# A rebuilt attention pipeline in front of a soft mixture of experts: head pairs, token-major output, wide loads, weights behind attention

## The chip, the cores and the metric

One core of one Trainium2 chip. The metric is the device time of one execution in microseconds (us), of which medians are quoted. For one core a run counts as slow when it is more than 1.5% above the fastest of the same kernel.

## The reference, cut to what matters

Attention over 8 batches and 8 heads, 576 tokens of 64 elements, with 16 extra "beacon" keys that every token sees. Its result is laid out as 4,608 tokens of 512 and goes through a soft mixture of experts: every token is dispatched to 32 slots (8 experts of 4 slots), and each token's output is a mix of all 32 slots.

```python
k_all = np.concatenate([beacon_k, k], axis=2)          # 16 + 576 keys
scores = (1 / np.sqrt(D)) * np.matmul(q, k_all.transpose(0, 1, 3, 2))
scores = np.where(causal, -1e9, scores)                # beacons are never masked
a = softmax(scores)
x = np.matmul(a, v_all).transpose(0, 2, 1, 3).reshape(B * S, H * D)   # 4608 x 512

logits = x @ phi                                       # 4608 x 32
slot_input = softmax(logits, axis=0).T @ x             # 32 x 512
for e in range(8):                                     # 4 slots per expert
    h = np.maximum(slot_input[e] @ w1[e], 0.0)         # 512 x 1024
    slot_out[e] = h @ w2[e]                            # 1024 x 512
out = softmax(logits, axis=1) @ slot_out               # 4608 x 512
```

q, k and v are drawn with a scale of 0.1, so the scores are near zero and the softmax is nearly uniform.

## The kernel before: the parts that the argument touches

All matmuls of attention work on q and k with the head's 64 elements on the partitions, so q and k, which are loaded with tokens on the partitions, are transposed by TensorE. The transposes land in PSUM, and VectorE copies them to SBUF. Two heads (a pair) share one such tile, one on partitions 0 to 63 and one on 64 to 127.

```python
# loads: tokens on partitions, one row of 64 floats (256 B) per token and head
nc.sync.dma_start(out=qs[s][0:rows, i, :, :],
                  in_=q[b, :, i * P:i * P + rows, :].rearrange("h p d -> p h d"))
# ... (k, v and the beacons alike)

for (st, dstT, nch) in ((qs[sb], qTp, NQC), (ks[sb], kTp, NCH)):
    tp = ps_tr.tile([P, nch * P], BF, name="trps", tag="trps")
    for c in range(nch):                       # five transposes of 128 x 128
        hi = st[:, c, hA:hB + 1, :].bitcast(BF).rearrange("p a b -> p (a b)")[:, 1::2]
        nc.tensor.transpose(tp[:, c * P:(c + 1) * P], hi, idb[:, :])
    nc.vector.tensor_copy(out=dstT[:, 0:nch * P], in_=tp[:, :])     # L196: flat on both sides

# ... scores, exp (ScalarE), causal mask (GpSimd) ...

avps = ps_av.tile([P, 1024], FP, name="av", tag="av")
# ... output of attention, transposed: 65 partitions (64 elements and the sum), tokens along columns
nc.tensor.matmul(avps[0:DD, ocol:ocol + w], vsh[sb][:, c, hh, :], expT[:, o:o + w],
                 start=(jj == 0), stop=(jj == len(grp) - 1))                      # L236
# ... copied to SBUF, transposed back by TensorE, divided by the sum

# ... the experts: all weights are loaded after attention
```

The parameters are F = 1,024 for the experts; `BF` is bf16, `F16` fp16 and `FP` fp32.

The softmax here doesn't subtract the row's maximum and nothing guards it: scores larger than these inputs give would overflow.

Of the kernel before, what the change touches and what calls it, by code (L numbers as in the profile page):

```python
# [8 lines left out]
DBG = {}  # L10


def _dbg(nc, name, ap):
    if DBG.get("on"):
        t = nc.dram_tensor(f"dbg_{name}", ap.shape, ap.dtype, kind="ExternalOutput")
        nc.sync.dma_start(out=t.ap(), in_=ap)
        DBG[f"dbg_{name}"] = True


FP = mybir.dt.float32  # L20
F16 = mybir.dt.float16
AL = mybir.AluOpType
AF = mybir.ActivationFunctionType


@with_exitstack
def kernel(
# [12 lines left out]
    nc = tc.nc  # L40
    P = 128

    B, H, S, D = q.shape
    Nb = beacon_k.shape[2]
    SK = S + Nb
    NCH = (SK + P - 1) // P
    SKPAD = NCH * P
    NQC = (S + P - 1) // P
    SQPAD = NQC * P
    Sl = S - (NQC - 1) * P  # L50
    DD = D + 1
    XDD = DD + (DD % 2)
    XT0, XT1 = 704, 1472
    scale = 1.0 / (D ** 0.5)

# [3 lines left out]
    N = out.shape[0]  # L59
    NDC = Dm // P  # L60
    NFC = F // P
    assert Dm == H * D and N == B * S

    SQS = [0, 288, 432, 512, S]
    rects = []
    halves = []
    off = 0
    for hhi in range(len(SQS) - 1):
        a, bnd = SQS[hhi], SQS[hhi + 1]
        ecb = off  # L70
        poff = 0
        idxs = []
        for c in range(NCH):
            sq0 = max(a, max(0, P * c - Nb))
            if sq0 >= bnd:
                continue
            w = bnd - sq0
            idxs.append(len(rects))
            rects.append((c, sq0, w, off, hhi, poff))
            off += w  # L80
            poff += w
        halves.append((idxs, poff, ecb))
        assert poff <= 512
    EXPW = off
    qk_pieces = [(c, hhi, po_, po_ + w, sq0)
                 for (c, sq0, w, o, hhi, po_) in rects]
    half_exp_regions = [[(0, pw, ecb)] for (_i, pw, ecb) in halves]

    mask_regs = []
    for (c, sq0, w, o, hhi, po_) in rects:  # L90
        C = sq0 + Nb - P * c
        if C < 128:
            mw = min(w, 128 - C)
            if mw > 0:
                mask_regs.append((o, mw, C, hhi))

    AVS = 288
    av_spans = [(0, 0, AVS), (512, AVS, S)]

    nchunks = []  # L100
    for b in range(B):
        for i in range(NQC):
            cnt = P if i < NQC - 1 else Sl
            nchunks.append((b, i, b * S + i * P, cnt))

    const = ctx.enter_context(tc.tile_pool(name="const", bufs=1))
    xpool = ctx.enter_context(tc.tile_pool(name="xpool", bufs=1))

    idf = const.tile([P, P], FP, name="idf")
    make_identity(nc, idf)  # L110
    idh = const.tile([P, P], F16, name="idh")
    make_identity(nc, idh)
    idb = const.tile([P, P], mybir.dt.bfloat16, name="idb")
    make_identity(nc, idb)
    ones32 = const.tile([P, 1], FP, name="ones32")
    nc.vector.memset(ones32[:, :], 1.0)
    ones32h = const.tile([P, 1], F16, name="ones32h")
    nc.vector.memset(ones32h[:, :], 1.0)
    phif = const.tile([P, NDC, NSL], FP, name="phif")
    nc.sync.dma_start(out=phif[:, :, :],  # L120
                      in_=moe_phi.rearrange("(c p) e -> p c e", p=P))
    phih = const.tile([P, NDC, NSL], F16, name="phih")
    nc.vector.tensor_copy(out=phih[:, :, :], in_=phif[:, :, :])

    xb = [xpool.tile([P, NQC, H, D], F16, name=f"x_{b}") for b in range(B)]
    eLh = xpool.tile([P, N], F16, name="eLh")
    dsum9 = xpool.tile([P, N // 512], FP, name="dsum9")
    xTes = ExitStack()
    xtp = xTes.enter_context(tc.tile_pool(name="xtp", bufs=1, side="right"))
    xT = [xtp.tile([P, N], F16, name=f"xT_{t}") for t in range(NDC)]  # L130

    with tc.tile_pool(name="stag", bufs=1) as stag, \
         tc.tile_pool(name="pairp", bufs=3) as pairp, \
         tc.tile_pool(name="headp", bufs=3) as headp, \
         tc.tile_pool(name="ps_sc", bufs=4, space=bass.MemoryType.PSUM) as ps_sc, \
         tc.tile_pool(name="ps_av", bufs=1, space=bass.MemoryType.PSUM) as ps_av, \
         tc.tile_pool(name="ps_tr", bufs=2, space=bass.MemoryType.PSUM) as ps_tr:

        qs = [stag.tile([P, NQC, H, D], FP, name=f"qstag{i}") for i in range(2)]
        ks = [stag.tile([P, NCH, H, D], FP, name=f"kstag{i}") for i in range(2)]  # L140
        vs = [stag.tile([P, NCH, H, DD], FP, name="vstag", tag="vstag") for i in range(2)]
        vsh = [stag.tile([P, NCH, H, DD], F16, name=f"vstagh{i}") for i in range(2)]
        oTs = [stag.tile([P, SQPAD], F16, name=f"oT{i}") for i in range(2)]
        vs = [vs[0], vs[0]]
        for i in range(2):
            nc.vector.memset(oTs[i][:, S:SQPAD], 0.0)
            nc.vector.memset(qs[i][64:P, NQC - 1, :, :], 0.0)
            nc.vector.memset(ks[i][64:P, NCH - 1, :, :], 0.0)
            nc.vector.memset(vs[i][:, :, :, D], 1.0)
            nc.vector.memset(vs[i][64:P, NCH - 1, :, :], 0.0)  # L150
            nc.vector.memset(vs[i][64:P - (SKPAD - SK), NCH - 1, :, D], 1.0)

        def stage_batch(b):
            s = b % 2
            for i in range(NQC):
                rows = P if i < NQC - 1 else Sl
                nc.sync.dma_start(
                    out=qs[s][0:rows, i, :, :],
                    in_=q[b, :, i * P:i * P + rows, :].rearrange("h p d -> p h d"))
            nc.sync.dma_start(out=ks[s][0:Nb, 0, :, :],  # L160
                              in_=beacon_k[b].rearrange("h n d -> n h d"))
            nc.sync.dma_start(out=vs[s][0:Nb, 0, :, 0:D],
                              in_=beacon_v[b].rearrange("h n d -> n h d"))
            for c in range(NCH):
                lo = max(0, c * P - Nb)
                hi = min(S, (c + 1) * P - Nb)
                if lo >= hi:
                    continue
                p0 = lo + Nb - c * P
                nc.sync.dma_start(  # L170
                    out=ks[s][p0:p0 + hi - lo, c, :, :],
                    in_=k[b, :, lo:hi, :].rearrange("h p d -> p h d"))
                nc.sync.dma_start(
                    out=vs[s][p0:p0 + hi - lo, c, :, 0:D],
                    in_=v[b, :, lo:hi, :].rearrange("h p d -> p h d"))
            nc.vector.tensor_scalar(out=vsh[s][:, :, :, :], in0=vs[s][:, :, :, :],
                                    scalar1=1.0, scalar2=None, op0=AL.mult)

        stage_batch(0)
        lg_done = [0]  # L180
        for b in range(B):
            if b + 1 < B:
                stage_batch(b + 1)
            sb = b % 2
            for g in range(H // 2):
                hA, hB = 2 * g, 2 * g + 1
                qTp = pairp.tile([P, SQPAD], mybir.dt.bfloat16, name=f"qT_{b}_{g}", tag="qT")
                kTp = pairp.tile([P, SKPAD], mybir.dt.bfloat16, name=f"kT_{b}_{g}", tag="kT")
                BF = mybir.dt.bfloat16
                for (st, dstT, nch) in ((qs[sb], qTp, NQC), (ks[sb], kTp, NCH)):  # L190
                    tp = ps_tr.tile([P, nch * P], BF, name="trps", tag="trps")
                    for c in range(nch):
                        hi = st[:, c, hA:hB + 1, :].bitcast(BF).rearrange(
                            "p a b -> p (a b)")[:, 1::2]
                        nc.tensor.transpose(tp[:, c * P:(c + 1) * P], hi, idb[:, :])  # L195
                    nc.vector.tensor_copy(out=dstT[:, 0:nch * P], in_=tp[:, :])  # L196
                expTs = {}
                for (hh, po) in ((hA, 0), (hB, 64)):
                    expTs[hh] = headp.tile([P, EXPW], F16, name="expT", tag="expT")
                for hhi, (idxs_, pw, ecb) in enumerate(halves):  # L200
                    sct = {}
                    for (hh, po) in ((hA, 0), (hB, 64)):
                        scps = ps_sc.tile([P, 512], FP, name="sc", tag="sc")
                        sct[hh] = scps
                        for (c, hx, plo, phi_, sqlo) in qk_pieces:
                            if hx != hhi:
                                continue
# [91 lines left out]
    with tc.tile_pool(name="moe", bufs=1) as moe, \  # L299
# [20 lines left out]
        for _e in range(3):  # L320
            fetch_expert(_e)
# [133 lines left out]
```

## Time and profile before

| what | before |
|---|---|
| median of 3 runs | 468.28 us (466.35 to 468.69) |
| attention, 32 head pairs | 19 to 340 us of a span of 464.3 |
| experts, with the load of all weights | 340 to 424 us |
| output | 424 to 464 us |
| DMA packets under 512 B | 115,744 of 132,682 |

The page's first part gives each engine's busy time, its share of the span and its instructions. PE is TensorE, PEld its weight loads, DVE is VectorE, ACT is ScalarE and POOL is GpSimd. For the kernel before:

```profile
PE 353.5 (76%) x3360; PEld 234.2 (50%) x3360; DVE 235.1 (51%) x849; ACT 156.2 (34%) x319; POOL 115.2 (25%) x522
```

The chain of waits, followed back from the last instruction, by engine and then by line, of the kernel before:

```profile
PE 65%; ACT 12%; DVE 10%; issue 6%; SPq 3%; POOL 1%; DMA 1%; DVEq 0%; ACTq 0%; POOLq 0%
PE av L236 19%; PE sc L208 17%; ACT expT L216 8%; PE sop L391 5%; PE trps L195 4%; PE av L250 4%; PE hps L371 4%; PE lgps L290 3%; PE fps L411 3%; PE xttr L281 3%; ACT osb L419 3%; ACT hsb L380 2%; POOL expT L222 1%; DVE w1h_5512 L313 1%; DVE w1h_5510 L313 1%
```

The table of stages gives the busy time of each engine in a stretch of time, the granted TensorE clock (1.00 is full speed), the busy share of the DMA engines and what they moved. The stretches are attention, the start of the weight loads, the rest of the experts, and the output; the kernel before:

```profile
core 0: us, PE busy (x) PEld busy (x) DVE busy (x) ACT busy (x) POOL busy (x), PEclk, DMA share, GB/s
20.00:340.00 320.00, 271.63 (x2996) 203.37 (x2995) 172.73 (x686) 122.37 (x272) 113.67 (x512) 0.63 0.39 89
340.00:358.00 18.00, 15.42 (x78) 5.97 (x78) 12.62 (x44) 1.69 (x4) 0.00 (x0) 1.00 1.03 411
358.00:424.00 66.00, 41.56 (x184) 14.19 (x185) 32.07 (x28) 7.09 (x7) 0.00 (x0) 0.77 0.87 347
424.00:464.00 40.00, 19.82 (x72) 8.20 (x71) 11.48 (x72) 23.38 (x36) 0.00 (x0) 0.55 0.63 236
```

In attention TensorE is busy 85% of the time (271.6 of 320 us), at a mean clock of 0.63, and no other engine reaches 55%. TensorE bounds this stage. DMA is idle for more than half of it, and the weights come only after it, at 411 GB/s with the DMA full.

VectorE's copies of the transposed q and k, two of them in the view of one line (columns: duration in ns as minimum/median/maximum, the first and last start in us, the shape):

```profile
L196 DVE COPY qT_0_177<-trps x1: 492/492/492, 9.1 to 9.1; 128x640 bf16<-128x640 bf16 x1
L196 DVE COPY kT_1_324<-trps x1: 480/480/480, 18.8 to 18.8; 128x640 bf16<-128x640 bf16 x1
```

A flat copy of 640 two-byte elements per partition from PSUM to SBUF takes 0.48 us. There are two per pair.

### The profile page before, as it was taken

How to read it: one execution, taken by the hardware profiler on the slowest of the kernel's cores; microseconds unless marked ns; L12 is line 12 of the kernel's file. 1: busy time of each engine (PE TensorE's matmuls, PEld its weight loads, DVE VectorE, ACT ScalarE, POOL GpSimd, SP SyncE). 2: the span in 40 equal slices, each digit the busy share in tenths (PEclk: the TensorE clock that was granted, in tenths of full speed). 3: DMA queues.
4: the chain of work that ended last, by engine and by line, in shares of the span. 5: the costliest groups of instructions: out<-in, count | busy, mean ns of one | idle time of the engine just before them, and what ended most of it. 6: DMA issues, size and time to landing. Idle time of an engine off the chain costs nothing.

```text
span 464.3 us, 8865 instructions
## 1 busy us (share of the span) xinstructions
PE 353.5 (76%) x3360; PEld 234.2 (50%) x3360; DVE 235.1 (51%) x849; ACT 156.2 (34%) x319; POOL 115.2 (25%) x522
## 2 busy tenths in 40 slices
PE   2597699988988888897897898895798566665563
PEld 1376576666666666666676666664333212222221
DVE  3244544465464465566665546445456644472331
ACT  1254233334343343435434334441010011003663
POOL 1253242224243243344434424331000000000000
PEclk9995555566665585579576567557589966769555
DMA  8993093077067086077260000000499999960776
GB/s 191 234 235 76 6 230 81 0 156 159 1 145 168 1 189 124 2 158 157 56 154 1 3 1 1 1 1 0 183 388 414 413 416 416 416 250 18 266 275 256
DMA packets 132682, 72.46 MB, mean 156 GB/s; under 512 B 115744, under 2 KB 115744, under 8 KB 132640
## 3 DMA queue, kind: packets, MB, share of 16 engines
q1 hardware_dynamic: 132640, 71.90, 52.1%
q8 instruction: 26, 0.43, 0.4%
q14 instruction: 16, 0.13, 0.1%
HBM read 62.46 MB, written 9.44 MB: 155 GB/s over the span
## 4 chain that ended last, share of the span: by engine, by line
PE 65%; ACT 12%; DVE 10%; issue 6%; SPq 3%; POOL 1%; DMA 1%; DVEq 0%; ACTq 0%; POOLq 0%
PE av L236 19%; PE sc L208 17%; ACT expT L216 8%; PE sop L391 5%; PE trps L195 4%; PE av L250 4%; PE hps L371 4%; PE lgps L290 3%; PE fps L411 3%; PE xttr L281 3%; ACT osb L419 3%; ACT hsb L380 2%; POOL expT L222 1%; DVE w1h_5512 L313 1%; DVE w1h_5510 L313 1%
## 5 line engine op out<-in xcount | busy, mean ns | idle before, releaser
L216 ACT ACTIVATE expT<-sc 128x496 f16<-128x496 f32 (+3 forms) x256 | 117.9, 519 | 187.2 <-PE av L236 129.0
L222 POOL TENSOR_SCALAR_AFFINE_SELECT expT<-expT 128x64 f16<-128x64 f16 (+5 forms) x512 | 113.7, 261 | 201.6 <-ACT expT L216 201.5
L236 PE MATMUL av<-expT,vstagh_125 128*65 128x64 f16 (+6 forms) x544 | 47.6, 259 | 3.7 <-DVE x_84 L269 2.5
L236 PE MATMUL av<-expT,vstagh_126 128*65 128x64 f16 (+6 forms) x544 | 47.2, 261 | 3.4 <-DVE xT_99 L283 1.4
L236 PEld LDWEIGHTS <-vstagh_125 128*65 128x65 f16 x544 | 42.3, 153 | 9.7 <-issue 4.8
L236 PEld LDWEIGHTS <-vstagh_126 128*65 128x65 f16 x544 | 42.8, 155 | 8.4 <-PE xttr L281 2.8
L243 DVE CAST oT_128<-av 65x288 f16<-65x288 f32 x32 | 14.5, 454 | 47.2 <-PE av L236 47.0
L380 ACT ACTIVATE hsb<-hps 4x1024 f16<-4x1024 f32 x8 | 8.1, 1013 | 71.7 <-PE hps L371 55.7
L243 DVE CAST oT_127<-av 65x288 f16<-65x288 f32 x32 | 14.5, 454 | 34.5 <-PE av L236 34.5
L411 PE MATMUL fps<-soh,eLh 32*128 32x512 f16 x36 | 19.7, 551 | 14.6 <-ACT osb L419 13.7
L419 ACT ACTIVATE osb<-fps,rc 128x512 f32<-128x512 f32 x36 | 23.4, 686 | 14.9 <-PE fps L413 6.8
L371 PEld LDWEIGHTS <-siT 128*4 128x4 f16 x64 | 5.5, 95 | 24.9 <-DVE w1h_5510 L313 6.8
L195 PE MATMUL trps<-idb,qstag_119 128*128 128x128 bf16 x80 | 10.6, 268 | 8.0 <-DMA qstag_119<-in_q_dram 7.6
L416 DVE TENSOR_SCALAR rc<-fps 128x1 f32<-128x1 f32 x36 | 5.7, 157 | 21.5 <-PE fps L413 20.7
L195 PE MATMUL trps<-idb,kstag_121 128*128 128x128 bf16 x80 | 10.9, 262 | 7.0 <-DMA kstag_121<-in_k_dram 6.2
L250 PE MATMUL av<-idh,oT_127 65*128 65x65 f16 x160 | 13.5, 230 | 3.1 <-DVE oT_127 L245 3.0
L250 PE MATMUL av<-idh,oT_128 65*128 65x65 f16 x160 | 12.8, 223 | 2.8 <-DVE oT_128 L245 2.8
L293 ACT ACTIVATE eLh<-lgps 32x512 f16<-32x512 f32 x9 | 5.3, 584 | 28.1 <-PE lgps L290 28.1
L245 DVE CAST oT_127<-av 65x288 f16<-65x288 f32 x32 | 14.2, 444 | 0.0
L245 DVE CAST oT_128<-av 65x288 f16<-65x288 f32 x32 | 14.2, 444 | 0.0
L250 PEld LDWEIGHTS <-oT_127 65*128 65x128 f16 x160 | 9.4, 118 | 7.3 <-DVE oT_127 L243 2.3
L283 DVE COPY xT_100<-xttr 128x128 f16<-128x128 f16 (+1 forms) x40 | 8.4, 211 | 8.4 <-PE xttr L281 8.1
(559 smaller groups left out, 592.8 us busy)
## 6 DMA issues: line engine op xcount, KB each, us to landing
out_dram<-osb SPq DMA_DIRECT2D x9, 1024.0 KB, 4.3
w1s_5506<-in_moe_w_dram SPq DMA_DIRECT2D x4, 2048.0 KB, 9.9
w2s_5508<-in_moe_w_dram SPq DMA_DIRECT2D x4, 2048.0 KB, 12.8
w1s_5507<-in_moe_w_dram SPq DMA_DIRECT2D x4, 2048.0 KB, 10.8
w2s_5509<-in_moe_w_dram SPq DMA_DIRECT2D x4, 2048.0 KB, 13.0
vstag<-in_v_dram SPq DMA_DIRECT2D x24, 256.0 KB, 4.5
qstag_119<-in_q_dram SPq DMA_DIRECT2D x16, 256.0 KB, 4.6
qstag_120<-in_q_dram SPq DMA_DIRECT2D x16, 256.0 KB, 4.3
```

What stands on the lines that cost most here:

```text
L195: nc.tensor.transpose(tp[:, c * P:(c + 1) * P], hi, idb[:, :])
L208: nc.tensor.matmul(scps[:, plo:phi_], kTp[po:po + D, c * P:(c + 1) * P], qTp[po:po + D, sqlo:sqlo + (phi_ - plo)], start=True, stop=True)
L216: nc.scalar.activation(expT[:, elo:elo + (bhi - blo)], sct[hh][:, blo:bhi], AF.Exp, scale=scale)
L222: nc.gpsimd.affine_select(out=expT[:, mlo:mlo + mw], in_=expT[:, mlo:mlo + mw], compare_op=AL.is_ge, fill=0.0, base=C, pattern=[[1, mw]], ...
L236: nc.tensor.matmul(avps[0:DD, ocol:ocol + w], vsh[sb][:, c, hh, :], expT[:, o:o + w], start=(jj == 0), stop=(jj == len(grp) - 1))
L243: nc.vector.tensor_copy(out=oT[0:DD, sa0:sb0], in_=avps[0:DD, ob0:ob0 + (sb0 - sa0)])
L245: nc.vector.tensor_copy(out=oT[0:DD, sa1:sb1], in_=avps[0:DD, ob1:ob1 + (sb1 - sa1)])
L250: nc.tensor.transpose(xth[:, base:base + DD], oT[0:DD, i * P:(i + 1) * P], idh[0:DD, 0:DD])
L371: nc.tensor.matmul(hp[0:SPE, fh * 512:(fh + 1) * 512], siT[:, t, e * SPE:(e + 1) * SPE], w1h[se][:, t, fh * 512:(fh + 1) * 512], start=(t ...
L391: nc.tensor.matmul(sop[0:NSL, :], hTz[e % 2][:, t, :], w2h[se][:, t, :], start=(e == 0 and t == 0), stop=(e == E - 1 and t == NFC - 1))
L411: nc.tensor.matmul(fp_[:, 0:Dm], eLh[0:NSL, nbase:nbase + P], soh[0:NSL, :], start=True, stop=True)
L419: nc.scalar.activation(osb[:, j, :], fp_[:, 0:Dm], AF.Copy, scale=rc[:, 0:1])
```

## The change

The intent is to take work from TensorE, to use the idle DMA during attention, and to issue fewer and larger instructions.

- q and k of a head pair are loaded as one block. Partition p gets nine consecutive tokens, 2,304 B in one row, instead of nine rows of 256 B.
- Nine pairs of 64x64 transposes replace five of 128x128 for each of q and k. Since a partition holds consecutive tokens, transpose j yields the tokens j, j+9, j+18 and so on; the copy to SBUF puts them back in order.
- Scores and exponentials work on two PSUM banks (both heads) at once: four exponentials per pair.
- The attention output is computed with tokens on the partitions, so it needs no transposes back. Both heads accumulate in one tile.
- The routing (logits, dispatch) is cut into pieces and run between the pairs. Of the 32 weight pieces, 14 are loaded and 13 cast to fp16 during attention.
- The output is taken out of PSUM by ScalarE and VectorE together.

The diff, cut to its core (cuts marked with `...`):

```diff
-                nc.sync.dma_start(
-                    out=qs[s][0:rows, i, :, :],
-                    in_=q[b, :, i * P:i * P + rows, :].rearrange("h p d -> p h d"))
+            nc.sync.dma_start(
+                out=t[:, :, :],
+                in_=src[b, 2 * g:2 * g + 2].rearrange("h s d -> (h s) d").rearrange(
+                    "(p j) d -> p j d", j=J))                                  # J = 9
...
-                    for c in range(nch):
-                        ...
-                        nc.tensor.transpose(tp[:, c * P:(c + 1) * P], hi, idb[:, :])
-                    nc.vector.tensor_copy(out=dstT[:, 0:nch * P], in_=tp[:, :])
+            for j in range(J):
+                for po in (0, 64):
+                    hi = t[po:po + 64, j, :].bitcast(BF)[:, 1::2]
+                    nc.tensor.transpose(tp[po:po + 64, j, :], hi,              # L203
+                                        idb[po:po + 64, po:po + 64])
+            nc.vector.tensor_copy(                                             # L205
+                out=dst[:, Nb:Nb + S].rearrange("p (s j) -> p j s", j=J), in_=tp[:, :, :])
...
+    av = ps_av.tile([P, 2, 512], FP, name="av")                # one tile, both heads, made once
...
-                                nc.tensor.matmul(
-                                    avps[0:DD, ocol:ocol + w],
-                                    vsh[sb][:, c, hh, :],
-                                    expT[:, o:o + w], ...)
-                    ... copy, transpose back, divide ...
+                nc.tensor.matmul(                                              # L244
+                    av[0:m, a, i * DD:(i + 1) * DD],
+                    ex[n][0:kn, a, o:o + m],
+                    vh[b % 2][0:kn, c, h, :],
+                    start=(c == 0), stop=(c == i))
+        nc.vector.reciprocal(out=r5[:, :], in_=avv[:, :, D])                   # L251
+        nc.vector.tensor_tensor(out=xb[b % 2][:, :, h, :], ...)                # L252
...
+        if n + 1 < NP:
+            transp(n + 1)          # the copies of the next pair are issued ...
+        if n >= 1:
+            attend(n - 1, 0)       # ... ahead of the division of this one, on VectorE
...
+            if n % 2 == 1 and n >= 5 and wl < 16 + 3:
+                load_w(wl)         # one weight piece of 1 MB every second pair
```

## The prediction

> **What bounds the kernel now.** The page and the table of stages split the 464 us span: first score matmul at 19.0 us, attention to 340, experts to 424, output to 464.
> - Attention, 321 us for 32 head pairs, about 10 us each, is bound by TensorE: busy 86%, while DVE has 55%, ACT 38%, POOL 36%, DMA 0 to 57%. The granted clock there is 0.57 to 0.63. Successive matmuls start 240 ns apart for 288 columns, 1.2 columns/ns. Per pair, with routing, about 7 us of streaming at half clock; the rest waits: ACT's exps wait for the output matmuls (129 us in the waits).
> - Experts: DMA busy 0.87 to 1.03 at 411 GB/s; 33.6 MB of weights come only now.
> - Output: 36 ACTIVATEs of 0.69 us, about 1.1 us apart, 236 GB/s.
>
> **What the change does.**
> 1. Attention output token-major: 30 matmuls of 65 columns per pair instead of 3,328 + 650 columns, no copy of the transposed output. At half clock 54 ns each: 1.6 us against 3.3.
> 2. q/k transposes: 36 of 64x64. Couples lie on disjoint quarters of the array; estimate 75 ns (55 to 110) per couple: 1.35 us against 1.07.
> 3. Scores still about 1,680 columns per couple: 1.4 us.
> 4. Routing 5.4 us per batch: 1.35 us per pair.
> 5. ACT: four two-bank exps, estimated from 0.597 us per 512 and 0.579 per 496 as 0.83 ns/column + 0.17: 3.5 us per pair against 4.15. DVE about 3.7 us, POOL about 2.5 us.
> So TensorE needs 6.2 to 7.2 us per pair at half clock, 4.5 at full clock (then DVE and the exp chain limit). Output matmuls fill 128 columns instead of 65 and idle time shrinks, so I expect more full clock: mean 0.65 to 0.7. TensorE: Matmul & The Clock Gate (Trainium skill), Part 1, gives two states set by activity; the trace agrees (only 0.5 and 1.0, in multiples of 3.4 us), but not which work raises it. Estimate 5.5 us per pair, attention about 178 us against 321.
> 6. Loads: q/k rows become 2,304 B. DMA: Bandwidth & Descriptors, Specifications, asks for 512 B at line rate; the trace agrees (256 B packets 216 to 235 GB/s, weights 413). DMA is not the limit in attention.
> 7. Weights: 13 or 14 of 32 pieces are loaded and cast behind attention, 3 more wait in staging. The next load needs cast 13, whose ACT half stands behind expert 2's Relu, so DMA idles about 25 us. Then 15 pieces x 2.54 us = 38 us. Attention end to last expert: about 60 us including the last routing (9 us), against 84. Gain only 24 us.
> 8. Output: two evacuators, 0.7 us each per two tiles, so DMA-bound: 9.4 MB in about 28 us against 40.
> Start unchanged (19 us): phi is queued behind v, and DVE waits for it.
>
> Sum: 19 + 178 + 62 + 29 + about 10 for [...]slack = 298 us.
>
> **Prediction: 298 us, range 265 to 338.** Faster by over 2%: 0.98; within 2%: 0.01; slower: 0.01.
>
> **What shows it.** Period of L217's first score step: 5 to 6.5 us; mean ACTIVATE for 1,024 columns 1.0 us; transposes' couples 55 to 110 ns; DMA share near 0 for 20 to 30 us after the last pair, then 410 GB/s; output stage 26 to 30 us, queue-bound.
>
> **What would make it wrong.** Clock stays at 0.5 (about 325 us) or goes to 1.0 (about 255). The 64x64 transposes do not overlap (+20 us). Switching between array shapes costs more than the 0.05 to 0.1 us seen. Waits on the two transpose banks or DVE's strided copies (estimated 0.75 us).

## The result, and the profile after

| | before | after |
|---|---|---|
| median, 4 runs each | 468.49 us (466.35 to 471.81) | 441.77 us (439.78 to 443.31) |
| time per head pair in attention | about 10 us | 9.97 us |
| DMA packets under 512 B | 115,744 | 41,920 |

The time per pair of the kernel after, and of the experiments below, is the mean distance between the starts of the 1,024-column exponentials of successive pairs.

The ratio is 0.942 (95% interval 0.9375 to 0.9468). Ratios here and below are the mean time of one kernel's fast runs over the mean of the other's fast runs of the same rounds, so they are not quite the ratio of the medians quoted. The prediction of 298 us (265 to 338) was wrong by 144 us; only the direction was right.

The page's first part, the kernel after:

```profile
PE 232.1 (53%) x3512; PEld 162.5 (37%) x3512; DVE 276.0 (63%) x336; ACT 144.4 (33%) x206; POOL 72.3 (16%) x142
```

TensorE lost 121 us of work, as intended. VectorE gained 41 us, with less than half as many instructions. The chain of waits by engine and by line, the kernel after:

```profile
DVE 48%; PE 30%; DMA 13%; ACT 3%; SPq 2%; issue 2%; ACTq 0%
DMA wst<-in_moe_w_dram 9%; PE av L244 8%; DVE qT_132 L205 7%; DVE qT_131 L205 7%; DVE kT_134 L205 6%; DVE kT_135 L205 6%; DVE kT_136 L205 6%; DVE qT_133 L205 6%; PE sc_158 L217 4%; PE tr L271 4%; PE tr L286 4%; DMA out_dram<-osb 3%; PE tr L203 3%; PE av L426 2%; DVE xb_145 L252 2%; DVE xb_144 L252 2%
```

VectorE went from 10% of the chain to 48%, and line 205 alone, under six tile names, is 38%. The table of stages of the kernel after, with the start of the experts cut into two:

```profile
core 0: us, PE busy (x) PEld busy (x) DVE busy (x) ACT busy (x) POOL busy (x), PEclk, DMA share, GB/s
23.00:340.00 317.00, 174.33 (x3023) 135.89 (x3024) 231.36 (x267) 113.50 (x156) 67.66 (x129) 0.68 0.43 128
340.00:349.00 9.00, 7.20 (x103) 5.57 (x102) 3.59 (x14) 0.99 (x4) 0.00 (x0) 0.50 0.28 113
349.00:358.00 9.00, 8.14 (x109) 4.24 (x107) 3.29 (x6) 0.75 (x4) 0.00 (x0) 0.73 0.01 2
358.00:400.00 42.00, 19.71 (x200) 9.16 (x199) 10.74 (x13) 14.18 (x21) 0.00 (x0) 0.61 0.98 365
400.00:440.00 40.00, 20.33 (x44) 5.75 (x44) 15.31 (x21) 13.67 (x21) 0.00 (x0) 0.50 0.60 246
```

Attention still takes 317 us. TensorE is busy in 55% of it now, VectorE in 73%. Neither is full, so the two must be waiting for each other. The view of line 205 in the kernel after (columns as for line 196 above):

```profile
L205 DVE COPY qT_131<-tr x11: 2692/2706/2719, 18.1 to 312.4; 128x576 bf16<-128x576 bf16 x11
L205 DVE COPY kT_134<-tr x11: 2883/2895/2905, 20.4 to 314.8; 128x576 bf16<-128x576 bf16 x11
```

Here is the surprise. The copy moves 10% fewer elements than the one of before, and takes 2.7 to 2.9 us instead of 0.48. The two per pair are 5.6 us, and the prediction had 1.5. The table of waits (who waited for whom, us in total, times, the longest) shows what stood behind them in the kernel after:

```profile
PE av L244 <- DVE xb_144 L252: 69.5, 16, 5.1
PE av L244 <- DVE xb_145 L252: 62.9, 16, 5.0
```

TensorE waited 132 us for the division of an attention output, which itself takes half a microsecond. The chain in order of time (start in us, duration in us, what), in a stretch of one pair of the kernel after, shows why:

```profile
148.31 0.64 PE tr L203 x12
148.96 0.02 issue
148.98 2.72 DVE qT_133 L205
151.69 2.52 DVE kT_136 L205
154.22 0.04 DVE r_1850 L251
154.25 0.02 issue
154.27 0.50 DVE xb_145 L252
154.78 0.04 issue
154.82 1.04 PE av L244 x15
155.86 0.29 PE sc_158 L217 x2
```

The two copies are ahead of the first head's reciprocal and division in VectorE's queue. The second head's output matmuls wait for that division, although they write another bank, because both heads accumulate in one tile `av`. So transposes, both copies, division, output matmuls and the last scores run one after another in each pair, where the prediction let them overlap.

### The profile page after: what moved, and what is told of

Its sections match the earlier page's. It is cut to its first block, busy times and chain, and to the rows that moved or that the text cites. A ratio compares the mean times of both kernels' runs of the same rounds, so it can differ in the third digit from the quotient of the medians.

```text
span 440.4 us, 8110 instructions
## 1 busy us (share of the span) xinstructions
PE 232.1 (53%) x3512; PEld 162.5 (37%) x3512; DVE 276.0 (63%) x336; ACT 144.4 (33%) x206; POOL 72.3 (16%) x142
## 2 busy tenths in 40 slices
DMA packets 63715, 72.41 MB, mean 164 GB/s; under 512 B 41920, under 2 KB 41920, under 8 KB 62656
## 4 chain that ended last, share of the span: by engine, by line
DVE 48%; PE 30%; DMA 13%; ACT 3%; SPq 2%; issue 2%; ACTq 0%
DMA wst<-in_moe_w_dram 9%; PE av L244 8%; DVE qT_132 L205 7%; DVE qT_131 L205 7%; DVE kT_134 L205 6%; DVE kT_135 L205 6%; DVE kT_136 L205 6%; DVE qT_133 L205 6%; PE sc_158 L217 4%; PE tr L271 4%; PE tr L286 4%; DMA out_dram<-osb 3%; PE tr L203 3%; PE av L426 2%; DVE xb_145 L252 2%; DVE xb_144 L252 2%
## 5 line engine op out<-in xcount | busy, mean ns | idle before, releaser
L244 PEld LDWEIGHTS <-ex 128*128 128x128 f16 (+2 forms) x960 | 54.4, 133 | 142.2 <-issue 140.6
L223 ACT ACTIVATE ex<-sc_158 128x992 f16<-128x992 f32 x64 | 48.3, 755 | 142.2 <-PE sc_158 L217 142.2
L223 ACT ACTIVATE ex<-sc_157 128x1024 f16<-128x1024 f32 x64 | 63.0, 985 | 63.9 <-PE sc_157 L217 63.3
L225 POOL TENSOR_SCALAR_AFFINE_SELECT ex<-ex 128x1024 f16<-128x1024 f16 x32 | 35.2, 1101 | 248.7 <-ACT ex L223 248.7
L244 PE MATMUL av<-vh_140,ex 128*128 128x65 f16 (+2 forms) x480 | 30.3, 233 | 69.5 <-DVE xb_144 L252 69.5
L244 PE MATMUL av<-vh_141,ex 128*128 128x65 f16 (+2 forms) x480 | 29.2, 229 | 62.9 <-DVE xb_145 L252 62.9
L205 DVE COPY qT_132<-tr 128x576 bf16<-128x576 bf16 x11 | 29.8, 2709 | 11.4 <-PE tr L203 11.2
L205 DVE COPY qT_131<-tr 128x576 bf16<-128x576 bf16 x11 | 29.8, 2707 | 11.1 <-PE tr L203 10.9
L426 PE MATMUL av<-w2h,hTz 128*32 128x512 f16 x64 | 23.7, 537 | 21.5 <-ACT hTz L424 21.5
L205 DVE COPY qT_133<-tr 128x576 bf16<-128x576 bf16 x10 | 27.1, 2708 | 11.3 <-PE tr L203 11.1
L205 DVE COPY kT_134<-tr 128x576 bf16<-128x576 bf16 x11 | 31.8, 2895 | 0.0
L205 DVE COPY kT_135<-tr 128x576 bf16<-128x576 bf16 x11 | 31.8, 2894 | 0.0
L205 DVE COPY kT_136<-tr 128x576 bf16<-128x576 bf16 x10 | 28.9, 2894 | 0.0
L203 PE MATMUL tr<-idb,qf 64*64 64x64 bf16 x576 | 20.3, 229 | 0.0
L203 PE MATMUL tr<-idb,kf 64*64 64x64 bf16 x576 | 18.8, 221 | 0.4 <-DMA kf<-in_k_dram 0.4
L286 PE MATMUL tr<-xT,phih 128*32 128x288 f16 x64 | 16.6, 440 | 0.4 <-DVE xT L276 0.4
```

Source lines behind the costliest of these rows:

```text
L203: nc.tensor.transpose(tp[po:po + 64, j, :], hi, idb[po:po + 64, po:po + 64])
L205: nc.vector.tensor_copy(out=dst[:, Nb:Nb + S].rearrange("p (s j) -> p j s", j=J), in_=tp[:, :, :])
L223: nc.scalar.activation(ex[n][:, :, o:o + w], sc[:, :, 0:w], AF.Exp, scale=scale)
L225: nc.gpsimd.affine_select(out=ex[n][:, :, 0:512].rearrange("p a (c t) -> p a c t", c=4), in_=ex[n][:, :, 0:512].rearrange("p a (c t) -> p ...
L244: nc.tensor.matmul(av[0:m, a, i * DD:(i + 1) * DD], ex[n][0:kn, a, o:o + m], vh[b % 2][0:kn, c, h, :], start=(c == 0), stop=(c == i))
L286: nc.tensor.matmul(lp[0:NSL, 0:w], phih[:, t, :], xT[b][:, t, Nb + hf * w:Nb + (hf + 1) * w], start=(t == 0), stop=(t == NDC - 1))
```

## The experiments

Two questions came out of this: why the copy is slow, and why its slowness costs all of its time. For the first there were three theories:

- **W**: writing two-byte elements with a wide step costs this on any engine, always. The copy reads PSUM flat and writes with a step of 18 B (nine tokens).
- **P**: it is contention; the copy is slowed by what else uses the memories at the time.
- **S**: a step costs the same on either side, so moving it to the reading side would gain nothing.

For the second, the theory was that the shared accumulator puts VectorE and TensorE in series; the rival was that VectorE's load alone sets the pace and splitting the tile would bring little.

### p1_probe: the copy alone

After the kernel's own work, with no other engine at work, copies of each kind are made three times. They differ in the pattern, and some in the source or the engine. The last stores still drained during the first of them (L470 and L472); from L474 on the DMA was idle.

```diff
+    sj  = pbig[:, 0:576].rearrange("p (s j) -> p j s", j=J)     # the kernel's written pattern
+    tsj = pt[:, :, :].rearrange("p j s -> p s j")               # the step moved to the read
+    nc.vector.tensor_copy(out=pbig[:, 0:k * 256:k], in_=flat[:, 0:256])  # k = 1,2,4,8,9,16 (sketched)
...
+    nc.vector.tensor_copy(out=pbig[:, 0:576], in_=flat)         # L485
+    nc.vector.tensor_copy(out=sj, in_=pt[:, :, :])              # L487
+    nc.vector.tensor_copy(out=pbig[:, 0:576].rearrange(...), in_=tsj)     # L489, flat write
+    nc.vector.tensor_copy(out=sj, in_=psrc[:, :, :])            # L491, from SBUF
+    nc.scalar.activation(sj, pt[:, :, :], AF.Copy)              # L493
...
+    nc.gpsimd.tensor_copy(out=sj, in_=psrc[:, :, :])            # L499
```

> The changed kernel, then, after its own work, single copies measured alone, three of each: 256 two-byte elements from PSUM by VectorE with a destination step of 1, 2, 4, 8, 9 and 16 elements (2 to 32 bytes) and of 32 bytes in fp32; 576 elements contiguous, 576 in the kernel's pattern (18-byte step in the destination), 576 with the step on the PSUM side (128 bytes) and a contiguous destination, 576 in the kernel's pattern from SBUF; the same on ScalarE and GpSimd. Theory W, the step of the write makes the copy slow: the kernel's pattern stays near 2.4 to 2.7 us although nothing else runs, from PSUM and from SBUF alike; 256 elements take 0.3 to 0.4 us up to a step of 4 elements and about 1.1 to 1.3 us from 8 elements (16 bytes) on; with the step on the read side 0.7 us. Rival P, contention with GpSimd, PE or DMA during attention: alone, the kernel's pattern takes about 0.75 us. Rival S, any stepped access is slow, on either side: the step on the PSUM side also takes over 2 us.

Groups of instructions by shape in the probe kernel (columns: line, engine, operation, tiles, shape and count | busy us, mean ns of one | idle time before):

```profile
L499 POOL COPY pbig<-psrc 128x576 bf16<-128x576 bf16 x3 | 8.1, 2706 | 150.8 <-ACT pbig L497 150.7
L493 ACT ACTIVATE pbig<-tr 128x576 bf16<-128x576 bf16 x3 | 8.1, 2695 | 40.3 <-DVE pbig L491 40.2
L491 DVE COPY pbig<-psrc 128x576 bf16<-128x576 bf16 x3 | 8.0, 2683 | 0.1
L487 DVE COPY pbig<-tr 128x576 bf16<-128x576 bf16 x3 | 8.0, 2678 | 0.1
L476 DVE COPY pbig<-tr 128x256 bf16<-128x256 bf16 x3 | 3.9, 1288 | 0.1
L480 DVE COPY pbig<-tr 128x256 bf16<-128x256 bf16 x3 | 3.7, 1225 | 0.1
L489 DVE COPY pbig<-tr 128x576 bf16<-128x576 bf16 x3 | 2.3, 757 | 0.1
L474 DVE COPY pbig<-tr 128x256 bf16<-128x256 bf16 x3 | 2.2, 725 | 0.1
L485 DVE COPY pbig<-tr 128x576 bf16<-128x576 bf16 x3 | 1.4, 453 | 0.1
L472 DVE COPY pbig<-tr 128x256 bf16<-128x256 bf16 x3 | 1.3, 443 | 0.1
L470 DVE COPY pbig<-tr 128x256 bf16<-128x256 bf16 x3 | 0.9, 291 | 0.7 <-DMA out_dram<-osb 0.6
```

The lines of 256 elements have a written step of 2 B (L470), 4 B (L472), 8 B (L474), 16 B (L476) and 32 B (L480). What the reader is to see:

- The kernel's copy takes 2,678 ns alone (L487), so it is not contention: P falls. (In the kernel the k copies take 0.2 us more than that; why is not shown.)
- It is as slow from SBUF (L491), on ScalarE (L493) and on GpSimd (L499).
- With the step on the reading side and a flat write, the same permutation takes 757 ns (L489): S falls. The flat copy takes 453.
- The cost grows with the written step from 291 to 443, 725 and 1,288 ns at 16 B, and then stops growing (1,225 ns at 32 B).

W stands for the kernel's copy. The form that it expected of the cost did not come: 256 elements were to take 0.3 to 0.4 us up to a step of 8 B, and took 443 ns at 4 B and 725 at 8 B. The first of these rises is 0.59 ns per element, about what the stepped read costs (0.53), so it need not come from the write. Starts of successive copies were 1.31 us apart at 18 B for 256 elements and 2.71 us for 576, so one element costs (2.71 - 1.31) us / 320 = 4.4 ns. The probe kernel took 497.11 us in its one look, which says nothing, as the probes are in it.

The Trainium skill has a hint on this: its page "SBUF — State Buffer", Specifications (TRN2), says that SBUF works in lines of 16 bytes, wants at least two hits per line, and pays a penalty at each change of line. The point at which the cost stops growing agrees with that: at 16 B every element is on a line of its own. The page gives no size. What happens inside the memory at such a write these runs don't show. They show that a stepped write to SBUF is slow and a stepped read of PSUM is not; a stepped read of SBUF was not tried.

### a1_read_strided: the step moved to the reading side

```diff
-                out=dst[:, Nb:Nb + S].rearrange("p (s j) -> p j s", j=J), in_=tp[:, :, :])
+                out=dst[:, Nb:Nb + S].rearrange("p (s j) -> p s j", j=J),
+                in_=tp[:, :, :].rearrange("p j s -> p s j"))
```

The same elements go to the same places, in another order.

> The changed kernel with the step of the q and k copies moved from the SBUF write to the PSUM read (same values, right result). Theory W (the stepped write costs 2 us per copy, 64 copies, and the whole pair waits for it): the copies fall from 2.7 to 2.9 us to about 0.7 us, the kernel to 300 to 335 us. Rival S (a step on either side costs the same): copies stay over 2 us and the kernel at 440 us. Rival P (contention): copies stay over 2 us.

Measured: 302.70 us (300.28 to 303.25), ratio to before 0.646 (0.6365 to 0.6544), against 0.942 for the change as it came. One pair takes 5.57 us, and the prediction had 5.5. The mean clock is 0.80 where it was 0.67. The copies, by groups, in this kernel:

```profile
L205 DVE COPY qT<-tr 128x576 bf16<-128x576 bf16 x32 | 24.2, 755 | 25.8 <-PE tr L203 25.6
L205 DVE COPY kT<-tr 128x576 bf16<-128x576 bf16 x32 | 23.9, 748 | 0.1
```

The 64 copies became shorter by about 2.05 us each (2.71 - 0.755 and 2.90 - 0.748, averaged), together 131 us. The kernel became faster by 441.8 - 302.7 = 139 us. So nearly all the time that the prediction missed comes from the written step of these copies, and it lies on the critical path. The 8 us beyond the copies' own 131 may come from the higher clock; that is not shown.

### a2_contig_wrong: no step at all

```diff
-                out=dst[:, Nb:Nb + S].rearrange("p (s j) -> p j s", j=J), in_=tp[:, :, :])
+                out=dst[:, Nb:Nb + S].rearrange("p (j s) -> p j s", j=J), in_=tp[:, :, :])
```

The tokens come out in the wrong order; only the time is of interest.

> The q and k copies with no step on either side; the tokens come out in a wrong order, so the result is wrong on purpose. The floor of the copy: W expects 0.45 to 0.5 us per copy (the kernel before took 0.48 us for 640 elements) and 295 to 330 us, at most some us under the run with the stepped read; P expects the copies to stay slow.

Measured: 284.32 us (282.13 to 286.34), ratio 0.607 (0.5993 to 0.6156); the copies took 454 and 449 ns. The copies are as expected, the total is 11 us below the expected 295 to 330. So what is left of the permutation when it is done on the reading side costs 302.7 - 284.3 = 18 us. The scores are so near zero that a wrong order of tokens stays within the tolerance. A passed comparison is no proof of the order on this data; that a1 is right follows from its indices, which address the same elements as the kernel after.

### e1_dose: half the dose

Only k takes the read step of a1; q keeps the written step.

```diff
+            if f is qf:
                 nc.vector.tensor_copy(out=... "p (s j) -> p j s" ..., in_=tp[:, :, :])
+            else:
+                nc.vector.tensor_copy(out=... "p (s j) -> p s j" ...,
+                                      in_=tp[:, :, :].rearrange("p j s -> p s j"))
```

> Half the dose: the q copies keep the stepped write, the k copies take the stepped PSUM read. Theory W (every slow copy lies on the path that paces a pair): half of the 139 us between the changed kernel (441.8) and the run with both copies moved (302.7), so 365 to 378 us. Rival: the first slow copy is hidden behind TensorE and only the second shows, 305 to 340 us; or the loss comes from something else that both copies trigger together, then near 440 or near 303.

Measured: 377.24 us (375.33 to 377.73), ratio 0.803 (0.7957 to 0.811). That is 64.5 us less than the kernel after; half of 139 is 69.5. The copies of q and of k in this kernel:

```profile
L206 DVE COPY qT<-tr 128x576 bf16<-128x576 bf16 x32 | 86.8, 2711 | 35.6 <-PE tr L203 35.0
L209 DVE COPY kT<-tr 128x576 bf16<-128x576 bf16 x32 | 30.6, 957 | 0.0
```

The k copies take 957 ns here, not the 748 of a1; 32 times the 1.94 us that they lost is 62 us. The loss goes with the number of slow copies, as a serial cost does.

### a3_av_split: one accumulator tile per head, copies still slow

```diff
-    av = ps_av.tile([P, 2, 512], FP, name="av")
+    avs = [ps_av.tile([P, 512], FP, name=f"av{i}") for i in range(2)]
...
-                    av[0:m, a, i * DD:(i + 1) * DD],
+                    avs[a][0:m, i * DD:(i + 1) * DD],
```

As many banks are used as before; each head now has its own tile.

> The copies as in the changed kernel (slow), but the two heads' output accumulators are two tiles of one bank each instead of one tile of two banks. Theory F: in the changed kernel the second head's output matmuls wait for the normalisation of the first head's only because they share a tile, and that wait (132 us of PE's waits) puts the copies and the matmuls in series; without it the period falls from 10.2 us to VectorE's own work of about 7.7 us per pair: 350 to 385 us. Rival: the wait is a symptom, VectorE is the limit in any case: 430 to 445 us.

Measured: 393.33 us (391.12 to 394.39), ratio 0.840 (0.8314 to 0.8482). This missed the expected 350 to 385 by 8 us, and the rival's 430 to 445 by far more. The wait of the output matmuls for the division is gone from the table of waits. It had been 132 us, and yet only 441.8 - 393.3 = 48 us were gained. The table of stages tells where the rest went; the same 40 us of attention, first in the kernel after, then with the tile split:

```profile
60.00:100.00 40.00, 21.76 (x398) 17.18 (x396) 29.58 (x35) 14.10 (x20) 8.17 (x17) 0.76 0.48 143
```

```profile
60.00:100.00 40.00, 26.27 (x453) 20.04 (x452) 35.38 (x40) 16.18 (x23) 10.74 (x21) 0.74 0.57 166
```

VectorE (third busy column) went from 74% to 88% of the stretch. Its own load, in the kernel after 231.4 us in attention or 7.2 us per pair, is now most of the 8.5 us that a pair takes. Both reasons are thus real: the series, and the load behind it.

### a5_read_avsplit and a5_again: both repairs together

The edits of a1 and a3 in one kernel. The second is the same kernel again, on another chip, because three of the four runs of the first were slow.

> The stepped read and the two accumulator tiles together. Theory F says that the shared tile still costs where the copies are fast: PE waits 33 us for the first head's normalisation in the run with the stepped read alone, so 280 to 292 us. Rival: with fast copies other waits take its place, 298 to 303 us. With the slow copies the split was worth 48 us.

> The same kernel as a5_read_avsplit, timed again because the earlier four runs spread (268.5 once, 274 to 276 three times) and the profile was classed slow: 268 to 276 us.

Measured: 274.94 us median for the first, but its fast runs are one of 268.49, so it gives no ratio. Again: 270.98 us (268.63 to 273.01, three fast), ratio 0.570 (0.5642 to 0.5761). This is better than the 280 to 292 us expected of the first. One pair takes 4.71 us. The wait that the split removes had been, in a1:

```profile
PE av L245 <- DVE xb L253: 33.0, 32, 1.8
```

The gain over a1, in another batch, is 302.7 - 271.0 = 32 us, about the size of this wait; 27 us of it lie between the first and the last pair. With slow copies the split gave 48 us of a wait of 132 us, as VectorE was nearly full; with fast copies it gave about all of it. The two gains don't add: 139 + 48 is 187, and together they gave 171.

### c1_rows256: narrow loads instead of the permutation

The permutation exists only because of the wide loads. This kernel loads each head with rows of 256 B, so that the transposes come out in order, and copies flat as in a2; its result is right.

```diff
-                in_=src[b, 2 * g:2 * g + 2].rearrange("h s d -> (h s) d").rearrange(
-                    "(p j) d -> p j d", j=J))
+            for a in range(2):
+                nc.sync.dma_start(out=t[64 * a:64 * a + 64, :, :],
+                                  in_=src[b, 2 * g + a].rearrange("(j p) d -> p j d", p=64))
```

> q and k are loaded in rows of 256 bytes, one head on each half of the partitions, 64 tokens a step, so that PSUM holds the tokens in order and the copy has no step on any side (right result, shared accumulator tile as in the changed kernel). It moves the price of the reordering to the DMA. If the contiguous loads of the change were needed: the DMA must move 28.3 MB at about 225 GB/s (126 us) and 14 MB of weights (35 us) in an attention stage of some 165 us, so the DMA binds and the kernel takes 300 to 330 us. If not: as the run with the contiguous copy in the wrong order, 282 to 292 us. In no case 440 us.

Measured: 322.81 us (320.54 to 327.02, three of four fast), ratio 0.687 (0.680 to 0.6939), 20 us slower than a1, and 38 us slower than a2 with the same flat copies (both of another batch). A stretch of attention of this kernel in the table of stages:

```profile
60.00:100.00 40.00, 28.75 (x638) 22.52 (x636) 19.56 (x55) 22.80 (x34) 13.20 (x26) 0.81 1.07 214
```

The DMA is full (a share of 1.07) at 214 GB/s, with 116,672 of 130,276 packets under 512 B. The Trainium skill's page "DMA: Bandwidth & Descriptors", Specifications, asks for 512 B at least for line rate; this agrees, as the weights' large packets moved at 411 GB/s. So the wide loads are worth 20 us even with the read step paid, but not with the written step. In the kernel before the same narrow loads kept the DMA busy for only 39% of attention, and TensorE set the pace there; what they cost it was not measured.

### b1_tail: the gap behind attention

The stages of the kernel after show DMA at 0.28 and then 0.01 from 340 to 358 us: after the last pair, loading weights stops for want of free buffers. b1 is a5 with the missing loads and casts issued before the last pair's work, and with ScalarE's part of the later casts given to GpSimd, which is idle there.

```diff
+        if last:
+            while wl < 17:
+                load_w(wl)
+                wl += 1
+            while wc < 16:
+                cast_w(wc, nc.gpsimd)
+                wc += 1
+                load_w(wl)
+                wl += 1
...
-            cast_w(wc, nc.scalar, 1280, 2048)
+            cast_w(wc, nc.gpsimd, 1280, 2048)
```

> a5_read_avsplit, and in addition the casts of weight pieces 13 to 15 go to GpSimd in the last iteration, and later casts to VectorE and GpSimd instead of VectorE and ScalarE, so that no load waits for a cast behind an expert's Relu. My step 7 said that the DMA idles about 25 us after the last pair for that reason: expected 15 to 25 us less than a5_read_avsplit, 260 to 275 us. Rival: the tail is bound by the experts' matmuls, then within 5 us of a5_read_avsplit.

Measured: 261.42 us (259.80 to 263.65), ratio 0.558 (0.5523 to 0.5636). The total is as expected, the gain is not: it is 7 us against the one fast run of a5 in the same batch (268.49) and about 9 against the fast runs of a5_again in another, where 15 to 25 us were expected; the total fits because a5 itself was faster than expected. From the last pair's first exponential to the end it took 93 us in this profile and 104 in that of a5_again. So the rival's bound of 5 us is passed, but not by much. The edit moves loads and changes the engine of casts; which of the two matters is not shown.

After the last pair the DMA stands nearly still for 5 us only (a share of 0.04 from 165 to 170 us) and then goes on. From 180 us, in the table of stages:

```profile
180.00:200.00 20.00, 17.70 (x262) 10.41 (x261) 9.87 (x17) 1.48 (x7) 8.83 (x7) 0.80 0.87 323
200.00:230.00 30.00, 16.94 (x131) 6.97 (x130) 9.65 (x12) 2.53 (x6) 13.35 (x9) 0.64 0.73 278
```

Attention of this kernel, two stretches of the same table:

```profile
20.00:60.00 40.00, 35.47 (x859) 27.09 (x854) 29.66 (x68) 32.52 (x43) 20.18 (x38) 1.00 0.99 269
100.00:140.00 40.00, 32.53 (x768) 25.05 (x763) 29.43 (x70) 27.60 (x40) 19.46 (x34) 0.92 0.99 282
```

TensorE is busy for 81 to 89% at nearly the full clock, and the DMA is full; v is still loaded in rows of 256 B. The DMA was as full in a5_again (1.04 and 0.99 in two such stretches) and less so in a1 (0.93 falling to 0.77 by 180 us). Which of the two engines sets the pace of b1 is not shown.

### b2_start: the small load that everything waits for

b1 starts its scores at 19.7 us, because VectorE's first copy after its setup waits for `phi` (8.0 us, to 15.0 us), which is queued behind v. b2 moves that load of 64 KB to the front.

```diff
+    phif = const.tile([P, NDC, NSL], FP, name="phif")
+    nc.sync.dma_start(out=phif[:, :, :], in_=moe_phi.rearrange("(c p) e -> p c e", p=P))
     load_pair(0)
     ...
-    phif = const.tile([P, NDC, NSL], FP, name="phif")
-    nc.sync.dma_start(out=phif[:, :, :], in_=moe_phi.rearrange("(c p) e -> p c e", p=P))
```

> b1_tail with the load of phi moved from behind the v loads to the front of the queue, since VectorE waits for phi before anything else of its work (first load-bound wait at the start 8 us). First score matmul at about 15 to 18 us in place of 23 us in the changed kernel, total 253 to 260 us. Rival: DMA is busy through the whole start and attention, so what is gained at the start is lost later in waiting for v: within 2 us of b1_tail (261.4).

Measured: 256.83 us median of four; two fast runs of 254.50 and 254.54, two slow of 259.11 and 259.50; ratio 0.537 (0.5328 to 0.5416). The timeline (start us, us, engine, line, what) of b2 at its first score matmul:

```profile
11.49 1.02 PE L219 MATMUL sc<-qT,kT 64*128 64x128 bf16 x14 [0.94 <-DVE kT L206]
```

The scores start 8 us earlier than in b1, sooner than the 15 to 18 us expected. By the fast runs 7 us of that reach the end (261.4 to 254.5); those are two runs, and b1 ran in another batch. The rival, that the gain is lost later in waiting for v, is not ruled out: the kept profile is of a slow run (259.11), in which a pair takes 4.90 us against 4.67 in b1, the last pair starts only 1.3 us earlier, and the loads of v are 25% of the chain against 8%. No trace shows a fast run of b2. It is the fastest version measured.

| version | median us | ratio to before |
|---|---|---|
| before | 468.49 | 1 |
| after | 441.77 | 0.942 |
| a3: accumulators split | 393.33 | 0.840 |
| e1: k repaired | 377.24 | 0.803 |
| c1: 256 B rows, flat copies | 322.81 | 0.687 |
| a1: q and k repaired | 302.70 | 0.646 |
| a5 again: a1 and a3 | 270.98 | 0.570 |
| b1: and the weights' gap closed | 261.42 | 0.558 |
| b2: and phi loaded first | 256.83 | 0.537 |

The medians of c1 and a5 again each include one slow run of four, that of b2 two; the ratios include none.

## Why the prediction was wrong

Its sum, stage by stage, against the profiled run of the kernel after (span 440.4 us):

| stage | predicted | measured | difference |
|---|---|---|---|
| to the first score matmul | 19 | 23.4 | +4 |
| attention | 178 | 317 | +139 |
| last pair to the end of the experts | 62 | 68 | +6 |
| output | 29 | 33 | +4 |
| slack | 10 | none separate | -10 |

- **The step that failed is step 5**: "DVE about 3.7 us" per pair, in which, as the last sentence of the prediction says, "DVE's strided copies" were "estimated 0.75 us". They took 2.71 and 2.90 us, and VectorE's load per pair was 7.2 us. With copies of 0.75 us (a1) the kernel takes 302.7 us, 5 us from the prediction. The prediction gives no working for the 0.75 us; it fits a step that costs no more than the loss of VectorE's doubled rate. The Trainium skill's page "VectorE: DVE Perf Modes", The perf-mode tier table, allows a copy from PSUM up to twice the plain rate, and the probe agrees on that: 453 ns flat, 757 ns with a step on the reading side. The estimate was right for a stepped read, and the kernel makes a stepped write. The note on 16-byte lines in the SBUF page was there to be read, and would have put the figure in doubt. The trace of before could not show it, as its copies of q and k are flat.
- **A second error is in the same step.** It took the largest load of any engine as the time of a pair, so it supposed overlap. The shared accumulator put TensorE and VectorE in series: 132 us of waits. With fast copies it is worth 32 us, so this error was the smaller. The 5.57 us of a1 meet the predicted 5.5, and its total the predicted 298, partly by luck: without the series the same work takes 4.71 us.
- **The danger was named and not weighed.** Waits on strided copies were in the list of what would make the prediction wrong, yet the upper end of 338 us left no room for it. One copy whose access pattern had no counterpart in the trace ran 64 times on what became the busiest engine; twice its estimate would have been 48 us.
- **TensorE (steps 1 to 3)** was right in the main: 174 us of work in attention against 272. The 64x64 transposes overlap: at half clock the two of a couple start within 3 ns of each other and the next couple 53 ns later, where 55 to 110 were predicted. The 15 output matmuls of a head start 56 ns apart in the median, where 54 were predicted; the 1.04 us shown above includes the tail of the last.
- **Clock**: predicted 0.65 to 0.7, measured 0.68 in attention, by luck: the reason given was that idle time shrinks, and TensorE's idle share rose from 15 to 45%. With the same matmuls and faster copies it rose to 0.89 in attention of a1, so the low clock went with the waiting here. Waiting is not all of it: in the kernel before TensorE was busy for 85% at 0.63, in b1 for 89% at 1.00. What else sets the clock stays open.
- **ScalarE** was right: an exponential of 1,024 columns took 0.985 us in the mean, predicted 1.0.
- **Loads (step 6)**: small packets fell from 115,744 to 41,920, and DMA was not the limit in the kernel after (share 0.43). What the prediction did not see is that it fills up as soon as the copies are fast: a share of 0.81 in attention of a1 and of 0.98 in that of a5_again.
- **Weights (step 7)**: the gap was there, some 18 us at a DMA share of 0.28 and 0.01 where 20 to 30 were predicted; 68 us to the last expert where about 60 were predicted. b1 closes most of it for 7 to 9 us.
- **Output (step 8)**: 29.5 us from the first store, predicted 26 to 30. The 33 us in the table above count from the end of the experts.
- **Start**: 4 us later than predicted. Two slow copies stand before the first score matmul; with fast copies a1 starts at 19.0 us.

## What to carry to other kernels

Try the step of a permuting copy on the side that reads PSUM and write SBUF flat (here 757 ns instead of 2,678), and when a change introduces an access pattern that the trace of before does not contain, measure that one instruction before trusting a sum, or widen the range by a multiple of it. After costing each engine, follow one loop of work through the tiles that two engines share: two halves of one tile in separate banks waited for each other here, and a tile per half took no more banks. When a large change gives little, look first at which engine's share of the chain grew, and at the shape whose mean time changed there.

## What the Trainium skill lacked or had wrong

- "SBUF — State Buffer", Specifications (TRN2), names the penalty for changing lines of 16 bytes but gives no size. Here 576 two-byte elements written 18 B apart took 2,678 ns against 453 flat, 4.4 ns per element.
- The same page, in its note on cachelines under "Door 1: The DMA port swizzle", takes two hits per line for enough to reach full bandwidth. At a written step of 8 B, which is two elements per line, 256 elements took 725 ns, against 443 at 4 B and 291 flat. So two were not enough for two-byte writes here.
- The cost is not set by lines alone: 256 four-byte elements written 32 B apart took 617 ns (median of three), two-byte ones at the same step 1,225 ns. The SBUF page does not say that the cost differs with the size of the element at one step in bytes, and these runs don't explain it.
- None of the pages read says that the cost is the same on three engines: ScalarE took 2,695 ns, GpSimd 2,706 and VectorE 2,678 for the same stepped write.
- A step on the reading side was cheap: a read of PSUM with a step of 128 B took 757 ns on VectorE, and 650 ns on ScalarE, the same as its flat read. The "VectorE: DVE Perf Modes" page does not tell a stepped write from a stepped read in its times.
